# A gated scan feeding a two-level mixture of experts: the first fp32 job's transposes and first four matmuls set behind the sixth unit's ranking

## The chip, the cores and the metric

The kernel runs on one core of a Trainium2 chip. The metric is the device time of one execution in microseconds (us). Three executions of the kernel before took 760.2, 761.58 and 762.66 us; their median is 761.58 us. One further execution was profiled.

## The reference, cut to what matters

Four sequences of 3648 tokens with 256 channels go through a gated scan. Each of the 14592 results is routed to one of 4 groups and then to one of the 4 experts of that group (top 1 both times), and that expert's two-layer network is applied, scaled by the two softmax weights.

```python
sig = 1.0 / (1.0 + np.exp(-f_logit))
f = lower_bound + (1.0 - lower_bound) * sig
i = 1.0 - f
for t in range(S):
    h = f[:, t] * h + i[:, t] * x[:, t]
    y[:, t] = h
...
g_idx = argmax(x @ w_group);  g_w = softmax(...)[g_idx]
e_idx = argmax(x @ w_expert[g]);  e_w = softmax(...)[e_idx]
h = np.maximum(x @ w1[g, e], 0.0)
out = g_w * e_w * (h @ w2[g, e])
```

## The kernel before

**Phase 1, by units.** The tokens are cut into 29 units of 512 (the last is shorter). For unit u: ScalarE computes the gate, a tanh (`p1_tanh`, L211, instruction L218) and two affine steps that turn it into f (`p1_affine`, L228); VectorE multiplies the input by 1 - f (`p1_gate`, L265, for the early units; inside `p1_tb`, L244, for later ones) and scans each half of the channels (`p1_tb(u, 0)` and `p1_tb(u, 1)`, L255, 512 steps each). TensorE then computes the router's logits (`p1_router`, L302), ScalarE copies them (L307), TensorE turns them (L315) and ScalarE copies the result Lg (L316). VectorE picks group and expert in small steps called s1, s2 and f3, the last of which writes the one-hot tile oh16f (L406); ScalarE takes an exponential (`f4x`, L426); TensorE ranks the tokens within their experts by small matmuls (`f4`, L417, L418, L420); VectorE sums the exponentials (`s6`, L361 first) and forms the positions posi (`f5`, L431 and L433), after which ScalarE copies the running counts (L435). `p1_back` transposes the scanned unit on TensorE (L283, 8 transposes) and ScalarE copies it out into rows (L285, twice, and L287); GpSimd scatters the rows into per-expert lists in DRAM (L392, four per unit). The first eight units are ranked one by one, so "unit 5" is the sixth.

**Phase 2, by jobs.** A job applies one expert to some rows of its list. Its rows are loaded by SyncE (xr, L924), transposed on TensorE (L1007), copied by ScalarE (xh and xl, L1013), multiplied by w1 (`m1_step`; the first three jobs run in fp32 by `raw1`, L1041), passed through a ReLU (L1044) and multiplied by w2 (`m2_step`, `raw2`, L1076). One call of `m1_step` of the first job covers two of the eight hidden blocks: four fp32 matmuls of 128x256, each of which the profile shows as two records. The second products of the first job, and the transposes of the second job, are tied behind the ranking of unit 7 (`BEHIND[2] = 7`, `tc.issue_after(ranked[...])`).

**What orders the work.** Phase 1 is a list of thunks made by `p1_thunks`; marks are positions in that list. The order on SyncE's queue is that of the program throughout. On TensorE, VectorE and ScalarE it is that of the program only inside the block `tc.manual_schedule(...)` at the end of the function: there the thunks up to the mark "first" are run, and then the first job's preparation (its transposes with `keep_warm`, and the copies xh and xl). What is traced later (the loop over jobs, which calls the remaining thunks between the matmul steps by `bg_step`) is placed by a scheduler that works with a cost model and may also put it into gaps of the block. `tc.keep_in_program_order` ties one instruction behind the one traced before it on its engine; `pinned` does so for the tanh and the gate of units 8 to 10. Unit 11's input is loaded early (`LAST_AT`), and its tanh is not tied.

`keep_warm(bank, n)` issues n matmuls of bf16 128x128 whose result nobody reads; `job_xt` of the first job issues 12 ahead of its transposes. PSUM tiles with the tag "p" rotate over three banks and those with "m1" over three.

In the round u = 6 the thunks are, in this order: router(5), logits(5), gate(6), scan (6, 0), the binding of the group, tanh(7), s1, the exponential, s2, f3, the ranking f4, affine(7), back(5), s6, f5 with the reciprocals, the scatters, the mark "first", scan (6, 1), `place(6)` and `choose(6)`.

Of the kernel before, what the change touches and what calls it, by code (L numbers as in the profile page):

```python
# [30 lines left out]
FAST = 9  # L31
# [9 lines left out]
AHEAD = 3  # L41
STAGED = range(4, 8)
BEGIN = 6
BEHIND = {2: 7, 3: 7}
MT = -(-max(CAPS) // 128)
QUARTERS = (13, 14, 15)
# [6 lines left out]
def gated_scan_moe(ctx: ExitStack, tc, zx, lower, wroute, wexp, out, S):  # L53
# [151 lines left out]
        units[u] = {"z": zt[:, 0], "x": zt[:, 1]}  # L205

    def pinned(u, ins):
        if 8 <= u <= FAST + 1:
            tc.keep_in_program_order(ins)

    def p1_tanh(u):  # L211
# [233 lines left out]
    def p1_thunks(us, groups, parts):  # L445
        th, marks = [], {}
# [21 lines left out]
        def put(f):  # L468
            th.append(f or (lambda: None))
            if hasattr(f, "mark"):  # L470
                marks[f.mark] = len(th)
# [28 lines left out]
        for u in us + [us[-1] + 1]:  # L500
            seq = []
            if u <= FAST:
# [12 lines left out]
                if ending:  # L515
                    bind, bound, (s1, f4x, s2, f3, f4, s6, f5, s7s) = routing(u - 1)
                    if u - 1 == BEHIND[2]:
                        f4.mark = "ranked"
                    put(bind)
                    if u > BEGIN:  # L520
                        back(u - 1)
                    put(lambda u=u: p1_tanh(u + 1))
                    put(s1)
                    put(f4x)
                    if u > 1 and member[u - 2] == member[u - 1]:
                        back(u - 2)
                    put(s2)
                    put(f3)
                    put(f4)
                    wave(u, 1)  # L530
                    put(lambda u=u: p1_affine(u + 1))
                    back(u - 1)
                    put(bound)
                    put(s6)
                    put(f5)
                    for f in s7s:
                        put(f)
                    wave(u, 1)
                elif u > 7:
                    wave(u, 1)  # L540
                    back(u - 1)
                for m in [m for m, v in ROWS_AT.items() if u == v]:
                    f = lambda m=m: early_rows(m)
                    f.mark = m
                    put(f)
                if u == BEGIN:
                    f = lambda: None
                    f.mark = "first"
                    put(f)
                put(lambda u=u: p1_tb(u, 1))  # L550
                wave(u, 1 if u < FAST else 99)
                if u in cuts and u - 1 in ends:
                    put(lambda u=u: place(u))
# [267 lines left out]
    def make_job(kind, idx):  # L821
# [22 lines left out]
        j.wh, j.wl, j.st = {}, {}, {}  # L844
        j.hh, j.hl = {}, {}
        j.xh, j.xl = {}, {}
        return j

    def job_e(j):
# [103 lines left out]
    def job_xt(j, pi):  # L953
# [2 lines left out]
        c0 = b0 - j.chunks[ch][0]  # L956
        if j.raw:
            if j.idx == 0:
                keep_warm(bank("m2"), 12)
            j.xh[ch] = mo.tile([P, 2 * P], F32, name="xh", bufs=X_BUFS)  # L960
            j.xl[ch] = mo.tile([P, 2 * P], F32, name="xl", bufs=X_BUFS)
        elif c0 == 0:
            j.xh[ch] = mo.tile([P, KD, 2 * P], F16, name="xh", bufs=X_BUFS)
            j.xl[ch] = mo.tile([P, KD, 2 * P], BF16, name="xl", bufs=X_BUFS)
# [168 lines left out]
    def first_parts():  # L1133
# [10 lines left out]
            out += [(u, f) for f in fs]  # L1144
        return out

    thunks, marks = p1_thunks(list(range(NU)), GROUPS, first_parts())
    bgq = deque(thunks)
    done = [0]
# [82 lines left out]
    with tc.manual_schedule(engines={mybir.EngineType.PE, mybir.EngineType.DVE, mybir.EngineType.Activation}):  # L1232
        start_macro(len(PLAN))
        bg_to(marks["first"])
        for t in prep_thunks(macros[len(PLAN)][0]):
            t()
    pending = None
    for mi, mac in enumerate(macros):
        if mi < len(PLAN):
# [7 lines left out]
        for j in mac:  # L1247
            for ch in range(len(j.chunks)):
                for cs in j.cols[ch]:
                    m1_step(j, ch, cs)  # L1250
                    left -= len(cs)
                    bg_step(q, left - 2, len(cs))
                for pj, pc in ([pending] if pending else []) + ([(j, ch)] if j.raw else []):
# [75 lines left out]
```

## Time and profile before

| | |
|---|---|
| median of three executions | 761.58 us |
| the profiled execution, its own time | 760.23 us |
| its span in the profile | 758.4 us |
| TensorE busy | 718.3 us (95%) |
| VectorE busy | 531.1 us (70%) |
| ScalarE busy | 450.3 us (59%) |
| GpSimd busy | 296.0 us (39%) |

Between the span and the execution's own time lie 1.83 us that the trace does not cover. Times in the rows are counted from the start of the span. A granted clock of 1.00 stands for the upper level of TensorE's clock (2.4 GHz) and 0.50 for the lower (1.2 GHz).

### The profile page before, as it was taken

The page shows a single profiled execution, that of the slowest core. Times are in us where ns is not written, and L with a number is a line of the kernel's source. Part 1 is how long each engine was busy: PE and PEld are TensorE (multiplying, and loading weights), DVE is VectorE, ACT ScalarE, POOL GpSimd, SP SyncE. Part 2 cuts the span into 40 slices and gives each one's busy share as a digit, 9 for nine tenths or more (in the row PEclk, how much of TensorE's full clock was granted, in tenths as well). Part 3 has the DMA queues.
Part 4 walks back from the last instruction along what each step waited for, and adds up shares of the span by engine and source line. Part 5 has one row for each costly group of instructions (what it writes and reads, how often), then busy time and mean ns, then how long its engine had stood idle before and what let it go on. Part 6 is the DMA issues. An engine that isn't in the chain of part 4 may idle for free.

```text
span 758.4 us, 21398 instructions
## 1 busy us (share of the span) xinstructions
PE 718.3 (95%) x8115; PEld 638.5 (84%) x8115; DVE 531.1 (70%) x1155; ACT 450.3 (59%) x824; POOL 296.0 (39%) x273
## 2 busy tenths in 40 slices
PE   3669999999999999999999999999999999999995
PEld 1557888888888888898899899999899999999995
DVE  6998779999999985687455735463754675557652
ACT  6667778876886864445454534453544465556552
POOL 3656355566855663631122212222222222223223
PEclk9969999999999999999999999999999999999998
DMA  8988899998897854567885752424354455566521
GB/s 326 397 276 278 249 378 336 382 298 294 300 315 248 251 177 149 131 178 181 187 201 155 161 129 77 133 83 122 120 143 107 142 164 139 159 177 196 172 70 35
DMA packets 101384, 152.01 MB, mean 200 GB/s; under 512 B 60898, under 2 KB 70913, under 8 KB 98464
## 3 DMA queue, kind: packets, MB, share of 16 engines
q1 hardware_dynamic: 86752, 103.27, 47.3%
q0 software_dynamic: 11408, 30.02, 10.8%
q10 hardware_dynamic: 3120, 17.34, 6.8%
q8 instruction: 64, 1.05, 0.6%
q14 instruction: 40, 0.33, 0.2%
HBM read 112.66 MB, written 38.40 MB: 199 GB/s over the span
## 4 chain that ended last, share of the span: by engine, by line
PE 62%; DVE 19%; DMA 8%; issue 4%; ACT 3%; SPq 1%; POOL 1%; POOLq 0%; ACTq 0%; DVEq 0%
PE ps_m L1095 30%; PE ps_m L1063 6%; PE ps_m L1065 6%; PE ps_m L1064 6%; DVE h L255 4%; DVE w L951 4%; PE ps_p L1063 3%; DMA st<-in_wexp_dram 3%; PE ps_p L1065 3%; PE ps_p L1064 3%; DVE hl L1069 3%; DMA xs<-rows,posi 3%; PE ps_p L283 1%; DVE zt L244 1%; ACT w L949 1%
## 5 line engine op out<-in xcount | busy, mean ns | idle before, releaser
L1095 PE MATMUL ps_m<-w,hh 128*128 128x256 bf16 (+7 forms) x2480 | 304.2, 251 | 0.0
L1095 PE MATMUL ps_m<-w,hl 128*128 128x256 f16 (+3 forms) x1240 | 250.3, 251 | 0.0
L1095 PEld LDWEIGHTS <-hh 128*128 128x128 f16 (+4 forms) x2480 | 183.1, 99 | 21.2 <-issue 2.7
L1063 PE MATMUL ps_m<-xh,w 128*128 128x256 f16 (+10 forms) x782 | 187.4, 254 | 4.7 <-DVE hl L1069 4.7
L1065 PE MATMUL ps_m<-xh,w 128*128 128x256 f16 (+10 forms) x782 | 187.2, 254 | 0.0
L1064 PE MATMUL ps_m<-xl,w 128*128 128x256 bf16 (+10 forms) x782 | 187.2, 254 | 0.0
L392 POOL DMA_INDIRECT xs<-rows,posi x114 | 141.1, 1238 | 111.3 <-ACT rows L287 25.6
L951 DVE TENSOR_TENSOR w<-st,w 128x1024 bf16<-128x1024 f32 x116 | 140.1, 1219 | 52.8 <-ACT w L949 52.5
L1109 POOL DMA_INDIRECT out_dram<-o,info x71 | 83.7, 1179 | 233.2 <-ACT o L1107 203.1
L1069 DVE SCALAR_TENSOR_TENSOR hl<-ps_m,hh 128x512 bf16<-128x512 f32 (+9 forms) x166 | 109.7, 666 | 57.2 <-ACT hh L1068 56.9
L1068 ACT ACTIVATE hh<-ps_m 128x512 f16<-128x512 f32 (+9 forms) x166 | 97.4, 588 | 65.3 <-PE ps_m L1065 64.9
L949 ACT CAST w<-st 128x1024 f16<-128x1024 f32 x116 | 120.4, 1050 | 14.1 <-PE ps_m L1095 8.1
L1064 PEld LDWEIGHTS <-w 128*128 128x128 f16 x1088 | 106.5, 98 | 12.4 <-issue 5.4
L1063 PEld LDWEIGHTS <-w 128*128 128x128 f16 x1088 | 106.5, 98 | 8.4 <-issue 1.2
L1065 PEld LDWEIGHTS <-w 128*128 128x128 bf16 x1088 | 106.4, 98 | 7.1 <-issue 0.2
L1095 PEld LDWEIGHTS <-hl 128*128 128x128 bf16 (+3 forms) x1240 | 97.7, 99 | 10.1 <-issue 0.7
L1109 POOL DMA_INDIRECT out_dram<-o,meta x51 | 59.9, 1175 | 104.8 <-ACT o L1107 93.7
L1107 ACT ACTIVATE o<-ps_m,info 128x256 f32<-128x256 f32 (+4 forms) x71 | 31.6, 445 | 73.6 <-PE ps_m L1095 65.8
L1069 DVE SCALAR_TENSOR_TENSOR hl<-ps_p,hh 128x512 bf16<-128x512 f32 (+13 forms) x65 | 41.9, 644 | 42.4 <-ACT hh L1068 42.1
L1063 PE MATMUL ps_p<-xh,w 128*128 128x256 f16 (+17 forms) x306 | 71.5, 249 | 0.0
L1064 PE MATMUL ps_p<-xl,w 128*128 128x256 bf16 (+17 forms) x306 | 71.5, 249 | 0.0
L1065 PE MATMUL ps_p<-xh,w 128*128 128x256 f16 (+17 forms) x306 | 71.5, 249 | 0.0
(179 smaller groups left out, 821.1 us busy)
## 6 DMA issues: line engine op xcount, KB each, us to landing
st<-in_wexp_dram SPq DMA_DIRECT2D x116, 512.0 KB, 7.6
zt<-in_zx_dram ACTq DMA_DIRECT2D x16, 1024.0 KB, 7.4
xs<-blank SPq DMA_DIRECT2D x28, 258.0 KB, 8.0
zt<-in_zx_dram SPq DMA_DIRECT2D x6, 1024.0 KB
w<-in_wexp_dram SPq DMA_DIRECT2D x12, 512.0 KB, 9.6
st<-in_zx_dram SPq DMA_DIRECT2D x8, 512.0 KB, 13.6
xr<-xs SPq DMA_DIRECT2D x14, 258.0 KB, 3.2
xs<-rows,posi POOLq DMA_INDIRECT x114
```

The lines of the kernel that those rows point to most:

```text
L255: sn = nc.vector.tensor_tensor_scan(out=h[:, k, c0 - a:c1 - a], data0=ff[:, k, c0 - a:c1 - a], data1=uu[:, k, c0 - a:c1 - a], initial=init ...
L392: sc = nc.gpsimd.indirect_dma_start(out=xs_v[G["t0"] + t][:, :], out_offset=bass.IndirectOffsetOnAxis(ap=R["posi"][:, t:t + 1], axis=0), i ...
L949: nc.scalar.copy(j.wh[i], j.st[i])
L951: nc.vector.tensor_tensor(out=j.wl[i], in0=j.st[i], in1=j.wh[i], op=ALU.subtract)
L1063: nc.tensor.matmul(po, w1_at(j.wh, k, c), xh[:, k], start=(k == 0), stop=False)
L1064: nc.tensor.matmul(po, w1_at(j.wh, k, c), xl[:, k], start=False, stop=False)
L1065: nc.tensor.matmul(po, w1_at(j.wl, k, c), xh[:, k], start=False, stop=(k == KD - 1))
L1068: eviction[0] = nc.scalar.activation(hi, pv, AF.Relu).ins
L1069: nc.vector.scalar_tensor_tensor(out=j.hl[ch][:, cs[0]:cs[-1] + 1, 0:w], in0=pv, scalar=0.0, in1=hi, op0=ALU.max, op1=ALU.subtract)
L1095: nc.tensor.matmul(pm[i * q:i * q + n, 0:dw], h[ch][:, c, ts], w2_at(w, c)[:, i * dw:(i + 1) * dw], start=(c == 0 and s == 0), stop=(c == ...
L1107: nc.scalar.activation(o[s, 0:dw], pm[s, 0:dw], AF.Copy, scale=lt.bitcast(F32)[s, r, 1:2])
L1109: nc.gpsimd.indirect_dma_start(out=out_v[out_n[0]].rearrange("n (g d) -> (n g) d", g=g), out_offset=bass.IndirectOffsetOnAxis(ap=lt[s, r, ...
```

## The change

Three things are edited. First, in the round u = 6 the transposes and copies of unit 5 (`back(5)`) come ahead of tanh(7) instead of behind affine(7). Second, the mark "first" moves up to just behind affine(7), so that the first job's preparation, now with 20 dummy matmuls, is traced directly behind unit 5's ranking and affine(7); the thunks from s6 of unit 5 to scan (6, 1), and one new thunk, `first_step`, follow it up to a new mark "begin", all still inside the manual block. `first_step` runs the first `m1_step` of the first job (four matmuls and a ReLU), which the loop over jobs then leaves out. Third, `pinned` also covers unit 11.

```diff
+BACKS = 5
...
     def pinned(u, ins):
-        if 8 <= u <= FAST + 1:
+        if 8 <= u <= FAST + 2:
             tc.keep_in_program_order(ins)
...
                     put(bind)
-                    if u > BEGIN:
+                    if u > BACKS:
                         back(u - 1)
                     put(lambda u=u: p1_tanh(u + 1))
...
                     put(lambda u=u: p1_affine(u + 1))
+                    if u == BEGIN:
+                        f = lambda: None
+                        f.mark = "first"
+                        put(f)
                     back(u - 1)
                     put(bound)
                     put(s6)
...
+                put(lambda u=u: p1_tb(u, 1))
                 if u == BEGIN:
+                    put(first_step)
                     f = lambda: None
-                    f.mark = "first"
+                    f.mark = "begin"
                     put(f)
-                put(lambda u=u: p1_tb(u, 1))
...
             if j.idx == 0:
-                keep_warm(bank("m2"), 12)
+                keep_warm(bank("m2"), 20)
...
+    def first_step():
+        j = macros[0][0]
+        j.begun.append((0, j.cols[0][0]))
+        m1_step(j, *j.begun[-1])
...
         for t in prep_thunks(macros[len(PLAN)][0]):
             t()
+        bg_to(marks["begin"])
...
                 for cs in j.cols[ch]:
-                    m1_step(j, ch, cs)
+                    if (ch, cs) not in j.begun:
+                        m1_step(j, ch, cs)
```

## Rows read from the trace of the kernel before

**Rows 1.** Busy time by stretch: PE, PEld, DVE, ACT, POOL, clock, DMA share, GB/s

```profile
70.00:80.00 10.00, 10.00 (x67) 8.62 (x66) 9.91 (x18) 4.78 (x10) 6.71 (x5) 1.00 0.94 355
...
150.00:160.00 10.00, 10.00 (x105) 9.21 (x103) 10.00 (x23) 9.36 (x18) 5.61 (x4) 1.00 0.97 304
...
380.00:420.00 40.00, 40.00 (x416) 36.41 (x414) 22.66 (x37) 20.13 (x34) 8.23 (x8) 1.00 0.73 184
```

**Rows 2.** The same view, microsecond by microsecond

```profile
48.00:49.00 1.00, 0.69 (x2) 0.47 (x3) 0.96 (x2) 0.43 (x3) 1.00 (x1) 0.50 0.00 0
...
56.00:57.00 1.00, 1.00 (x5) 0.51 (x3) 1.00 (x3) 0.00 (x0) 0.69 (x2) 0.50 1.06 415
...
58.00:59.00 1.00, 1.00 (x10) 0.85 (x8) 0.75 (x2) 0.45 (x2) 0.82 (x1) 1.00 0.99 386
```

**Rows 3.** Timeline of PE: start, duration, line, operation, idle before and its releaser

```profile
48.31 0.47 PE L315 MATMUL ps_p<-ident,rs 128*128 128x128 f32 x1 [0.39 <-ACT rs L307]
48.71 0.71 PE L417 MATMUL ps_p<-runoff,row 1*128 1x80 f32 x2
52.13 0.21 PE L418 MATMUL ps_p<-oh16f,upto 128*128 128x64 bf16 x1 [2.71 <-DVE oh16f L406]
...
52.33 1.95 PE L283 MATMUL ps_p<-ident,h 128*128 128x128 f32 x8
54.07 1.49 PE L292 MATMUL ps_m<-upto,tri 128*128 128x128 bf16 x12
55.35 0.42 PE L1007 MATMUL ps_p<-ident,xr 128*128 128x128 f32 x1
...
57.97 0.70 PE L1041 MATMUL ps_m<-xh,w 128*128 128x256 f32 x2
...
58.62 1.04 PE L283 MATMUL ps_p<-ident,h 128*128 128x128 f32 x8
...
68.09 0.19 PE L418 MATMUL ps_p<-oh16f,upto 128*128 128x64 bf16 x1
```

**Rows 4.** Timeline of ACT, same columns

```profile
48.94 1.06 ACT L218 ACTIVATE st<-st 128x1024 f32<-128x1024 f32 x1
49.90 1.05 ACT L218 ACTIVATE zt<-zt 128x1024 f32<-128x1024 f32 x1
51.09 0.27 ACT L426 ACTIVATE ex<-ge 128x80 f32<-128x80 f32 x1
51.27 1.50 ACT L228 ACTIVATE st<-st,mid,half 128x512 f32<-128x512 f32 x2
...
53.46 0.59 ACT L285 COPY rows<-ps_p 128x512 f32<-128x512 f32 x1
...
57.48 0.38 ACT L1013 COPY xl<-ps_p 128x256 f32<-128x256 f32 x1
```

**Rows 5.** Timeline of DVE, same columns

```profile
49.59 1.27 DVE L255 TENSOR_TENSOR_SCAN h<-st,h 128x512 f32<-128x512 f32 x1
...
51.85 0.23 DVE L406 TENSOR_TENSOR oh16f<-oh 128x64 bf16<-128x64 f32 x1
52.00 0.23 DVE L361 TENSOR_REDUCE sm<-ex 128x20 f32<-128x80 f32 x1
...
52.89 1.21 DVE L265 SCALAR_TENSOR_TENSOR st<-st 128x1024 f32<-128x1024 f32 x1
...
57.44 1.21 DVE L244 SCALAR_TENSOR_TENSOR zt<-zt 128x1024 f32<-128x1024 f32 x1
...
59.07 0.24 DVE L329 TENSOR_REDUCE mx<-Lg 128x20 f32<-128x80 f32 x1 [0.32 <-ACT Lg L316]
```

**Rows 6.** The chain that ended last, just behind unit 7's ranking

```profile
68.37 0.58 PE ps_p L1007 x4
68.95 1.30 PE ps_m L1041 x6
```

**Rows 7.** Issues on SP's queue, the first job's rows

```profile
48.31 0.89 SPq L924 DMA_DIRECT2D xr<-xs  x2
```

More of the change, by code (lines that the diff above doesn't have):

```diff
@@ L846, in make_job @@
         j.xh, j.xl = {}, {}
+        j.begun = []
         return j
```

## The prediction

> **What bounds the kernel now.** I read the busy time by stretch first. Where a saving early on is worth anything is seen there: from 60 us on TensorE has no time to spare. It is busy for 10.00 of 10 us at 70 to 80, and for 40.00 of 40 at 380 to 420, where VectorE has 22.66; only between about 130 and 260 us is VectorE as full, 10.00 of 10 at 150 to 160, with the DMA engines at 0.97 [rows 1]. So a microsecond of TensorE work done earlier should come off the end, less what the VectorE stretch swallows.
>
> The timeline of TensorE comes next. Before 58 us the engine waits for phase 1: 2.71 us ahead of unit 5's ranking at 52.13, for oh16f [rows 3]. From there it runs without a gap: 8 transposes of unit 5, 12 dummies, the first job's transposes from 55.35, and the first real matmul of a job at 57.97 [rows 3]. The same view microsecond by microsecond shows the lower clock in all this: granted 0.50 at 48 to 49 and still at 56 to 57, and 1.00 at 58 to 59 [rows 2]. Between, at some 57.8, it rose, after TensorE had been busy for 5.6 us (57.8 - 52.13). Eight transposes took 1.95 us at the lower level and 1.04 at the upper [rows 3].
>
> The timelines of VectorE and ScalarE show who sets the pace up to 68 us. VectorE's chain from Lg of unit 6 at 59.07 [rows 5] to unit 7's ranking at 68.09 [rows 3] is 9.0 us long. That ranking is a gate: the first job's second products stand behind it. What TensorE still had to do of the first products when the gate opened is 1.30 us, beside 0.58 of the second job's transposes, which the gate holds too [rows 6].
>
> **The change part by part.** *Unit 5's transposes first.* They follow the logits (48.31 + 0.4 = 48.7) into a gap where TensorE waited anyway, and take 1.95 us at the lower clock: to 50.65. The first ranking matmuls (0.71) follow, to 51.3 [rows 3]. TensorE loses nothing by it.
>
> *Scan (6, 1) leaves the middle of s1.* The scheduler had put it there at 49.59 for 1.27 us [rows 5]. The pitch of such scans is 1.2, so oh16f comes at 51.85 - 1.2 = 50.65, done at 50.9, and the ranking runs at 51.3 instead of 52.13: 0.8 us earlier.
>
> *ScalarE's order.* It is the price. The second copy of unit 5's rows (0.59 long, one every 0.5) waits for the transposes' end at 50.65 and is over at 51.2. Only then comes tanh(7), which had started at 48.94 and takes 1.06: to 52.2. Unit 5's exponential, at 51.09 before, follows at 52.2, done at 52.45, and affine(7) (1.50) ends at 53.9 [rows 4]. The sum sm needs the exponential, so VectorE, done with oh16f at 50.9, stands until 52.45: 1.55 us idle where it had no gap. Behind sm (before: 52.00 to gate(7) at 52.89 [rows 5], plus 0.3 of two small steps that had slipped behind the gate) come 1.2 us to 53.7, then scan (6, 1) to 54.95, then gate(7), due at 52.89 before: 2.06 us later.
>
> *Unit 11 in its place.* Its tanh at 49.90 [rows 4] and gate of 1.21 at 57.44 [rows 5] leave this stretch. The gate goes into the stretch after 75 us; I cost it there at nothing, because TensorE is the full engine there and ScalarE has 4.78 of 10 us [rows 1]; if that cover is gone the price is 1.2 us. Here it gives 1.2 back. Unit 6's s1 then stands at 59.07 - 0.32 (the wait shown) + 2.06 - 0.3 - 1.2 = 59.3, or 0.2 later than before, if Lg is there by then.
>
> *Twenty dummies and the first job's transposes.* Twelve dummies go from 54.07 to 55.35, 0.107 us each [rows 3]; twenty take 2.14, from the ranking's end at 51.6 to 53.75. Four transposes take 0.98 at the lower clock, 0.5 at the upper. Their rows were issued by SP from 48.31 on, 0.89 long [rows 7], which leaves 4.5 us to land; that they had landed by 55.35 is all that the timeline of TensorE shows. The first job's weights lie ready: no DMA engine moved anything at 48 to 49 [rows 2]. The copies xh and xl (0.38, about 0.3 apart [rows 4]) follow to 55.25, and the first matmul can start on xh at about 54.95 instead of 57.97: 3.0 us earlier.
>
> *The clock.* TensorE is now busy without a gap from 48.31 on. [...] These take 8 records of 0.217 (1.30 for 6 [rows 6]), 1.73 us, and twice that, 3.46, at the lower level. I take the upper, because it is what the nearest row shows, and keep both.
> The Trainium skill's page "TensorE: Matmul & The Clock Gate" (Part 1: The HAM clock gate) says that the moment of the transition differs from run to run, because it depends on where the first matmul happens to land. By that rule the step costs 1.73 us in some executions and 3.46 in others. The rise at 57.8 is one instance here and cannot show it.
>
> *Four matmuls ahead of router(6).* With them, router(6) starts at about 56.7, Lg is out at 58.0, and s1 does not wait for it (59.3). At the lower clock they end at 58.4, router(6) at twice its time at 59.5, and Lg is out at 60.6.
>
> *GpSimd and SP.* No instruction is added to either. Unit 5's scatters need its copies and the reciprocals, about 1 us earlier than before; the second job's rows wait for them on SP, and its transposes for the gate at 68.09: worth nothing. On SP nothing changes places around the block.
>
> **The sum.** TensorE starts real matmuls 3.0 us earlier, but before the gate it has only 1.30 us of first products left to bring forward [rows 6]; the rest of the lead becomes idle time in front of the gate. The gate itself moves by the 0.2 of unit 6's s1, less some 0.4 that the chain lost to matmuls queued ahead of its rankings (of 0.32 in one wait and more of that size): -0.2, with bounds of -1.2 (one scan's pitch, if the scheduler leaves scan (8, 1) out of unit 7's s1 as well) and +1.4 (the lower clock in the item above: 60.6 + 0.1 against 59.3). Together -1.5. Of this I let the stretch with VectorE full swallow 0.3, between nothing and all of it: -1.2 us. The profiled execution had a span of 758.4 and took 760.23 us, so its like would take 759.0; it stands 1.35 below the median of the runs, and the forecast is made against the median: 761.58 - 1.2 = 760.4 us. A measurement of this kernel can tell about 0.3% from no change, 2.3 us, so this counts as the same.
>
> **Rivals.** *A: the gate comes early (faster).* With TensorE warm and the scheduler free to order anew, the whole lead of 3.0 us arrives at the gate. Then the time is about 761.58 - 3.0 = 758.6, up to 1 us less if scan (8, 1) leaves s1 too. For it: VectorE's chain is freed of unit 11, and units 6 and 7 are short of Lg (0.32). Against: the 1.55 us that VectorE stands. Chance 0.30.
>
> *B: the chain is the bound, and it is late (slower).* VectorE's stand of 1.55 us is not made good by unit 11's gate, because that work is wanted later, and the clock rises only after the four matmuls, so that router(6) stands behind 3.46 us of them. Then Lg comes at 60.6 and the gate by 1.5 later; with the 1.2 us of unit 11's gate wanted back in a full stretch it is +2.7: 764.3. It decides once unit 6's s1 starts later than about 60.6. For it: the lower clock up to 57.8. The rule of the page "TensorE: Matmul & The Clock Gate" of the Trainium skill (above) would give it in part of the executions. Against: VectorE's idle time after 75 us, while TensorE is full. Chance 0.18.
>
> *C: hidden anyway (same).* The first job's start is no bound at all: the stretch from 130 to 260 us is set by VectorE and the transfers, and the lead is idle time there: 761.6. For it: 10.00 of 10 us and 0.97 [rows 1]. Against: TensorE has no time to spare there either. Chance 0.12. That the change doesn't do what it says (the first four matmuls still after 57 us, because the copies xh and xl come late) ends here too.
>
> **How the numbers follow.** Forecast 0.40, A 0.30, B 0.18, C 0.12. Faster by over 0.3% is A, 0.30; within 0.3% is the forecast and C, 0.52; slower is B, 0.18. The range reaches from 757.4, A with most of what a scan adds, to 763.6, which leaves out the worse part of B; the forecast's own range is 759.3 to 761.8.
>
> **What would show it.** Right: the ranking of unit 5 near 51.3, VectorE idle for about 1.5 us ahead of sm near 52.4, twenty dummies to 53.8, a granted clock of 1.00 by 55, the first job's first matmul near 55, and TensorE idle ahead of unit 7's ranking at about 68. Wrong: sm not waiting for the exponential; a first matmul after 57; unit 7's ranking before 66.5 or after 69.5; or a difference between the two kernels that arises after 100 us, where the change touches nothing, from another order of the scheduler's.

## The result, and the profile after

The changed kernel takes 766.27 us (median of 19 runs, 761.22 to 770.65), the kernel before 760.84 beside it (19 runs, 759.36 to 763.23): a ratio of 1.007, 95% interval 1.0057 to 1.0084. It is slower by about 5.4 us. Its runs also scatter over 9.4 us, those of before over 3.9. The profiled execution took 766.32 us with a span of 764.5; all times below are of that one, unless another kernel is named. The kernel's lines carry numbers one to seven higher than before (L315 is now L316, L924 is L931, L1007 is L1014, L1041 is L1048).

Around the block the change does what it says. The timeline of PE, answering to [rows 3], with three stops from later on that the kernel before does not have:

```profile
47.41 0.47 PE L316 MATMUL ps_p<-ident,rs 128*128 128x128 f32 x1 [0.39 <-ACT rs L308]
47.67 1.91 PE L284 MATMUL ps_p<-ident,h 128*128 128x128 f32 x8
...
50.17 0.19 PE L419 MATMUL ps_p<-oh16f,upto 128*128 128x64 bf16 x1 [0.19 <-DVE oh16f L407]
...
50.31 1.28 PE L293 MATMUL ps_m<-upto,tri 128*128 128x128 bf16 x20
...
54.23 0.70 PE L1048 MATMUL ps_m<-xh,w 128*128 128x256 f32 x2
...
67.62 0.19 PE L419 MATMUL ps_p<-oh16f,upto 128*128 128x64 bf16 x1 [0.87 <-DVE oh16f L407]
...
68.98 1.35 PE L1083 MATMUL ps_m<-w,hh 128*128 128x256 f32 x5
...
112.88 0.74 PE L1014 MATMUL ps_p<-ident,xr 128*128 128x128 f32 x4 [2.30 <-ACT rows L286]
...
126.40 0.48 PE L1014 MATMUL ps_p<-ident,xr 128*128 128x128 f32 x2 [2.46 <-DMA xr<-xs]
128.29 1.10 PE L1014 MATMUL ps_p<-ident,xr 128*128 128x128 f32 x4 [1.41 <-ACT rows L288]
```

The transposes of unit 5 fill the gap, the first job's first matmul stands at 54.23 instead of 57.97, and the gate (unit 7's ranking) opens at 67.62 instead of 68.09 [rows 3]. What follows the gate in the chain that ended last is now

```profile
67.90 0.58 PE ps_p L1014 x4
...
69.05 2.36 PE ps_m L1083 x10
```

and the 1.30 us of first products that stood there [rows 6] are gone. The clock, microsecond by microsecond, answering to [rows 2]; granted clock, DMA share and GB/s are the last three columns:

```profile
49.00:50.00 1.00, 0.98 (x5) 0.59 (x4) 0.86 (x5) 0.83 (x3) 0.70 (x2) 0.70 0.53 145
50.00:51.00 1.00, 0.83 (x18) 0.83 (x19) 0.12 (x1) 1.00 (x2) 0.72 (x1) 1.00 0.40 136
```

It is at its upper level from 50 us on, and not at 57.8. ScalarE first, then VectorE, for [rows 4, 5]:

```profile
50.11 1.06 ACT L219 ACTIVATE st<-st 128x1024 f32<-128x1024 f32 x1
51.06 0.26 ACT L427 ACTIVATE ex<-ge 128x80 f32<-128x80 f32 x1
```

```profile
51.36 0.23 DVE L362 TENSOR_REDUCE sm<-ex 128x20 f32<-128x80 f32 x1 [1.24 <-ACT ex L427]
...
58.63 0.23 DVE L330 TENSOR_REDUCE mx<-Lg 128x20 f32<-128x80 f32 x1
```

So at 69 us the changed kernel leads by 1.77 us: the first of the first job's second products stands at 68.98, and in the kernel before at 70.75.

```profile
70.75 1.56 PE L1076 MATMUL ps_m<-w,hh 128*128 128x256 f32 x6
```

Of this lead 0.90 us is there already at the logits of unit 5 (47.41 against 48.31), ahead of everything that the change edits. In e6, a second trace of the changed kernel, these logits stand at 48.27, and the lead is 0.85 us (69.90).

**Where the time goes** is seen in the busy time by stretch, answering to [rows 1]: PE, PEld, DVE, ACT, POOL, clock, DMA share, GB/s.

```profile
70.00:80.00 10.00, 10.00 (x68) 8.44 (x67) 8.70 (x11) 7.74 (x16) 7.27 (x6) 1.00 1.02 345
...
110.00:120.00 10.00, 6.98 (x59) 5.58 (x58) 8.77 (x23) 8.34 (x17) 5.67 (x6) 1.00 1.03 414
120.00:130.00 10.00, 6.12 (x41) 5.04 (x40) 9.72 (x16) 9.26 (x16) 5.78 (x4) 0.90 1.01 371
```

and in the same stretches of the kernel before:

```profile
110.00:120.00 10.00, 10.00 (x74) 8.38 (x73) 8.69 (x23) 8.04 (x16) 7.54 (x7) 1.00 1.02 402
120.00:130.00 10.00, 9.47 (x102) 8.07 (x101) 9.16 (x19) 8.34 (x16) 4.55 (x4) 1.00 1.01 322
```

TensorE stands for 6.9 us between 110 and 130 (10 - 6.98 and 10 - 6.12), where it stood for 0.5 before. Setting the n-th of TensorE's matmuls of the jobs (6258 records in either trace) beside the n-th of the other trace tells when the loss is made. The one that starts at 97.4 us in the kernel before starts 1.83 us earlier in the changed one, so the lead is kept up to there; the one at 118.8 starts 0.5 us later, the one at 124.5 7.2 later, and from 146 us on it is 5.9 to the end. ScalarE's copies of the experts' products (into hh, hl and o; 371 in either trace) say the same from the 24th on: 6.2 us behind (139.36, 133.19), and 5.9 from the 45th (185.21, 179.27; the 301st 647.38, 641.42). Nothing is lost after 140 us. Part of it is the clock, which falls with the stops:

```profile
126.00:128.00 2.00, 0.48 (x2) 0.32 (x2) 1.86 (x5) 2.00 (x4) 0.54 (x1) 1.00 1.02 413
128.00:130.00 2.00, 1.71 (x8) 1.47 (x9) 2.00 (x3) 1.52 (x5) 1.22 (x1) 0.52 1.00 395
130.00:132.00 2.00, 2.00 (x14) 1.49 (x12) 2.00 (x5) 0.18 (x2) 0.00 (x0) 0.62 0.88 352
```

After 4.4 us with 0.48 of work (123.9 to 128.3) TensorE runs at a granted 0.52 and 0.62, and its records of 0.27 us take 0.42. At the upper level the busy time of the last two rows would have been 1.6 us shorter ((1 - 0.52) x 1.71 + (1 - 0.62) x 2.00).

The transposes that wait there belong to the fifth job, and what they wait for is its rows. Issues on SP's queue, after and then before (xr: rows of the third and fourth jobs at 82 us, of the fifth job and the next at 117 to 120; st: weights, the fourth job's first):

```profile
81.64 3.68 SPq L931 DMA_DIRECT2D xr<-xs  x4
90.18 1.48 SPq L684 DMA_DIRECT2D xs<-blank  x2
91.94 20.23 SPq L948 DMA_DIRECT2D st<-in_wexp_dram  x11
120.26 3.09 SPq L931 DMA_DIRECT2D xr<-xs  x4
```

```profile
82.00 3.56 SPq L924 DMA_DIRECT2D xr<-xs  x4
88.22 1.49 SPq L678 DMA_DIRECT2D xs<-blank  x2
89.97 19.39 SPq L941 DMA_DIRECT2D st<-in_wexp_dram  x11
116.74 3.10 SPq L924 DMA_DIRECT2D xr<-xs  x4
```

The transposes for which the fifth job's rows are used run without a stop in the kernel before:

```profile
122.44 0.88 PE L1007 MATMUL ps_p<-ident,xr 128*128 128x128 f32 x6
```

The rows of the third and fourth jobs are issued at the same time, but the blanks behind them, which must not overwrite what is still being read, come 2.0 us later, so do the weights behind the blanks, and the fifth job's rows come 3.5 later. SP stands 6.8 us for the scatters of units 8 and 9 before it issues these rows (6.1 before). GpSimd issues the last two of the eight at 107.34 and 109.38, against 105.24 and 107.17, after a stand of 5.06 us (4.23) for ScalarE. ScalarE's timeline, after and then before:

```profile
81.48 0.23 ACT L317 COPY Lg<-ps_p 128x80 f32<-128x80 f32 x1 [0.39 <-PE ps_p L316]
84.37 0.34 ACTq L205 DMA_DIRECT2D zt<-in_zx_dram  x1
84.76 1.06 ACT L219 ACTIVATE zt<-zt 128x1024 f32<-128x1024 f32 x1 [3.06 <-DVE oh L340]
...
88.33 0.35 ACT L427 ACTIVATE ex<-ge 128x160 f32<-128x160 f32 x1
```

```profile
79.85 0.33 ACTq L204 DMA_DIRECT2D zt<-in_zx_dram  x1
80.29 0.47 ACT L1107 ACTIVATE o<-ps_m,xr 128x256 f32<-128x256 f32 x1 [3.14 <-DMA w<-in_wexp_dram]
...
83.72 0.22 ACT L316 COPY Lg<-ps_p 128x80 f32<-128x80 f32 x1
...
86.47 0.35 ACT L426 ACTIVATE ex<-ge 128x160 f32<-128x160 f32 x1
```

ScalarE issues the input load of unit 13 from its own queue and stands in front of it for some 3 us in both kernels. Before, the stand ends at 79.85, when weights have landed, ahead of the logits of units 8 and 9 (83.72). In the changed kernel these logits are out 2.2 us earlier (81.48), but the stand lies right behind them, and the exponential comes 1.9 us later, 88.33 against 86.47. The records of the transfers in the traces say why. The transfers of SP and ScalarE between 60 and 127 us share eight semaphores (counters that tell that a transfer has landed), and a transfer waits for the one that had its semaphore before. In the kernel before the load of unit 13 has the semaphore of the last weights of the third job, issued at 66.37; in the changed kernel, whose transfers are issued in another order, it has that of the second of the third job's row transfers, which SP issues only at 82.21.

### The profile page after: what moved, and what is told of

It reads as the page before. It is cut to its first block, busy times and chain, and to the rows that moved or that the text cites. A ratio compares the mean times of both kernels' runs of the same rounds, so it can differ in the third digit from the quotient of the medians.

```text
span 764.5 us, 21414 instructions
## 1 busy us (share of the span) xinstructions
PE 719.1 (94%) x8123; PEld 638.3 (83%) x8123; DVE 531.3 (69%) x1155; ACT 450.1 (59%) x824; POOL 295.9 (39%) x273
## 3 DMA queue, kind: packets, MB, share of 16 engines
q8 instruction: 64, 1.05, 0.6%
## 4 chain that ended last, share of the span: by engine, by line
PE 63%; DVE 17%; DMA 6%; issue 5%; ACT 4%; POOL 2%; SPq 2%; POOLq 0%; DVEq 0%; ACTq 0%
PE ps_m L1102 30%; PE ps_m L1070 7%; PE ps_m L1071 6%; PE ps_m L1072 6%; DVE h L256 4%; PE ps_p L1070 3%; DVE w L958 3%; PE ps_p L1071 3%; PE ps_p L1072 3%; DMA st<-in_wexp_dram 2%; DVE hl L1076 2%; PE ps_p L284 2%; DMA out_dram<-o,meta 1%; DMA xs<-blank 1%; PE ps_m L1083 1%
```

## The experiments

Theories, as they were formed: **S**, ScalarE's stand at unit 13's load (at first called L); **P**, the tie of unit 11's tanh to program order; **W**, the start of the fourth job's weight casts; **O**, that the order of before is a lucky one; **X**, the chain from ScalarE over the scatters to the fifth job's rows; **D**, that from 100 us on the DMA engines are full, so what they leave undone before is missing later. Ratios are to the kernel before, timed in the same group of runs. The runs stand in five groups (e1 to e4, e5 to e8, e9 to e12, e13 to e16, e17 and e18); the kernel before takes 761 us in the second and the last and 780 to 784 us in the other three. A ratio is good within a group; times and traces are compared with those of before and after only in the groups at 761 us.

| run | what it is | before, us | ratio, 95% interval |
|---|---|---|---|
| e1_load13_early | change, unit 13's load early | 780.5 | 1.0034 (1.0010 to 1.0057) |
| e2_no_pin | change without the tie | 780.5 | 1.0080 (1.0048 to 1.0111) |
| e3_before_pin | before with the tie alone | 780.5 | 1.0075 (1.0048 to 1.0102) |
| e4_no_first_step | change, first four matmuls not moved | 780.5 | 1.0074 (1.0048 to 1.0099) |
| e5_before_control | before | 761.4 | 0.9999 (0.9984 to 1.0013) |
| e6_after_again | change | 761.4 | 1.0058 (1.0038 to 1.0078) |
| e7_before_load13_late | before, unit 13's load later | 761.4 | 1.0000 (0.9988 to 1.0012) |
| e8_step_only | first job's early start alone | 761.4 | 1.0033 (1.0018 to 1.0048) |
| e9_after_loads_on_sp | change, two loads on SP | 783.0 | 1.0030 (0.9999 to 1.0060) |
| e10_no_pin_loads_on_sp | the same without the tie | 783.0 | 1.0065 (1.0039 to 1.0091) |
| e11_before_loads_on_sp | before, two loads on SP | 783.0 | 0.9993 (0.9968 to 1.0019) |
| e12_after_loads_early | change, two loads early | 783.0 | 1.0077 (1.0049 to 1.0106) |
| e13_after_weights_first | change, weights ahead of blanks | 783.7 | 1.0076 (1.0049 to 1.0103) |
| e14_before_weights_first | before, weights ahead of blanks | 783.7 | 1.0023 (0.9991 to 1.0055) |
| e15_before_cast4_late | before, one weight cast later | 783.7 | 1.0017 (0.9987 to 1.0048) |
| e16_after_third | change | 783.7 | 1.0118 (1.0078 to 1.0158) |
| e17_before_scalar_held | before, ScalarE held 3.1 us | 761.5 | 1.0019 (1.0000 to 1.0039) |
| e18_load13_early_again | e1 again | 761.5 | 1.0044 (1.0025 to 1.0062) |

**One part taken out, or alone (e1 to e4, e8).**

```
e1   -  seq += [lambda u=u: (p1_load(u + AHEAD - 1), ...
     +  seq += [lambda u=u: ([p1_load(v) for v in ((12, 13) if u == 10 else (u + AHEAD - 1,))], ...
e2   -  if 8 <= u <= FAST + 2:          + if 8 <= u <= FAST + 1:
e3      the kernel before with FAST + 2, and nothing else
e4   -  put(first_step)                 + pass
e8      e2, and BACKS = 6 instead of 5
```

> The changed kernel with one line moved: the load of unit 13's input is traced one round earlier, together with unit 12's. In the built program it then stands ahead of the tanh of unit 11 on ScalarE's queue, and the transfer that it must wait for is a blank written at 67 us, no longer the rows of the third job. All edits of the change stay. Theory L (the load of unit 13 stands on ScalarE's queue behind the third job's rows, issued at 81.6 us and landed at 84.3, and holds up all that follows): the load goes out by 78 us, ScalarE no longer stands from 81.7 to 84.4, the fourth job's last weights are cast by 109 us instead of 112.3, TensorE is idle for under 2 us between 110 and 130 instead of 7, and the time is 757 to 761 us. Theory W (the early first job only empties TensorE's work sooner, and the transfers set the time) and theory P (unit 11's late tanh and gate cost it): nothing of theirs is touched, and the time stays at 764 to 768.

> The changed kernel without the third edit: the tanh of unit 11 is free again. The built program puts the load of unit 13 behind a blank written at 67 us. Theory P: the time comes back to 759 to 762, and with unit 11's tanh back at about 50 us the gate and the affine steps leave the stretch from 75 us on. Theory L: back to 757 to 761 too, because the load no longer waits for the third job's rows; the load goes out before 80 us. Theory W: stays at 764 to 768, because the first job starts just as early.

> The kernel before with the third edit alone (unit 11's tanh keeps its place). The built program puts the load of unit 13 behind unit 12's load, which goes out near 69 us. Theory P: slower by 4 to 6 us, 765 to 767. Theory L: 759 to 762, no loss, because the load does not wait for the third job's rows. Theory W: 760 to 762, as the first job starts as late as before.

> The changed kernel without the new thunk: the first four matmuls are left to the scheduler, all else stays (transposes ahead, twenty dummies, unit 11 tied). The built program puts the load of unit 13 behind unit 12's load. Theory L: 757 to 761, with the load out before 80 us. Theory P: 764 to 768. Theory W: the transposes and copies still come early and the scheduler puts the first matmuls right behind them, so it stays near 764 to 768.

> The changed kernel without the earlier transposes of unit 5 and without the tie on unit 11's tanh: the first job's start after unit 6's rank matmuls, with twenty dummies, is alone. Theory P (the tie on unit 11 costs) expects no loss: 0.997 to 1.001. A fourth theory, O (the order of before is a lucky one, and every other order of ScalarE's queue between 70 and 100 us costs about as much), expects 1.005 to 1.008, as with the pin alone and with the change without the pin.

No part carries the loss. The tie alone costs 0.75% (e3), the change without it 0.80% (e2), the change without the moved matmuls 0.74% (e4), the early start alone 0.33% (e8). These don't add up to 0.7%. P is not excluded as a part, but as the only cause it falls with e8, which has no tie. O predicted 1.005 to 1.008 for e8, and got less.

The traces add that e2, e3 and e4 lose time at another place than the changed kernel does. From the logits of unit 5 to the first of the first job's second products it is 21.57, 21.63 and 21.62 us in after, e6 and e18, 22.45 in the kernel before and 22.20 to 22.58 in the seven traces that start like the kernel before (before, e5, e7, e11, e14, e15, e17). In e2, e3 and e4 it is 24.02, 26.55 and 24.08, and in e12 and e16 further down 25.36 and 24.63: up to 4.1 us more than in the kernel before, ahead of 78 us, where the changed kernel gained. In e3 TensorE stands ahead of unit 6's logits, in e16 in front of the first real matmul:

```profile
62.40 0.33 PE L315 MATMUL ps_p<-ident,rs 128*128 128x128 f32 x1 [1.60 <-issue]
```

```profile
58.42 0.70 PE L1048 MATMUL ps_m<-xh,w 128*128 128x256 f32 x2 [2.59 <-ACT xh L1020]
```

Behind these stops the granted clock falls to 0.50 (from 64 to 68 us in e3, from 60 to 62 in e16). Why these executions stand there stays open. The ratios of these five runs hold this loss, as far as their one trace each tells, and say the less about the one between 110 and 130 us.

**Controls (e5, e6, e16).** The kernels before and after, unedited.

> The kernel before itself, for a trace on the chip on which the variants run. Every theory expects a ratio of 1.000. What is read from it: when unit 13's input load starts on ScalarE, when the exponential of units 8 and 9 runs, when the fourth job's weights are issued, and how long TensorE is idle between 110 and 140 us. If the theory holds that a chain from those units' logits to the fourth job's weights sets the time, all variants timed so far (ratios 1.003 to 1.008) must have the weights' casts 1.5 to 4 us later than this trace.

> The changed kernel itself beside its variants. Every theory expects about the ratio on record, 1.006 to 1.008. What is read from it: whether the load of unit 13 stands at the head of ScalarE's queue until the third job's rows have landed here too, and whether the loss of TensorE lies between 110 and 130 us again.

> The changed kernel beside these variants, for the comparison on the same chip. Every theory expects 1.006 to 1.008; W expects its fourth cast at 111 us or later.

e6 is the most telling trace, because the same program was slower: span 768.3 against 764.5. ScalarE's timeline names the transfer that it stands for:

```profile
87.52 0.33 ACTq L205 DMA_DIRECT2D zt<-in_zx_dram  x1
87.90 1.06 ACT L219 ACTIVATE zt<-zt 128x1024 f32<-128x1024 f32 x1 [5.27 <-DMA xr<-xs]
...
91.46 0.35 ACT L427 ACTIVATE ex<-ge 128x160 f32<-128x160 f32 x1
```

The stand is 2.2 us longer than in the first trace, the exponential 3.1 later, the fifth job's rows are issued at 122.39 (2.1 later), and TensorE stops for them for 3.91 us at 130.53 and runs at 0.50 to 0.57 until 136. The 45th copy is 3.2 us later, of which 0.9 are there already at the second products (69.90 against 68.98). The other 2.3 go with the chain X, within one program, in this one pair of executions. That the stand now hangs on a transfer that takes longer in one execution than in another also fits the scatter of the runs.

**The stand moved or imitated (e7, e17, e18).**

```
e7   before: p1_load(13) traced at u == 12 instead of 11
e17  before: + for _ in range(3 if u == 12 else 0):
             +     nc.scalar.copy(ff[:, :, 0:w], U["z"][:, :, 0:w])      (ahead of unit 12's tanh)
e18  e1 unchanged
```

> The kernel before with one thing changed: unit 13's input load follows unit 12's tanh on ScalarE's queue instead of going ahead of it. Theory L (the load of unit 13, and what waits for it, sets the time) expects a ratio of 1.002 to 1.005, since the load goes at least one tanh (1.06 us) later. Theory P (the work put ahead of the exponential of units 8 and 9 sets it) expects 1.000 to 1.002, since only one tanh changes its place. Theory W (the fourth job's weights set it) expects the ratio to follow the time at which these weights are issued: 1.000 if that has not moved, 1.005 or more if it is 2 us late.

> The kernel before with three copies of 1.05 us (unit 12's gate input onto itself) ahead of unit 12's tanh on ScalarE: ScalarE is held about 3.1 us ahead of the exponential of units 8 and 9, as by the stand at unit 13's load in the changed kernel; which load waits for which transfer stays as it was, and so do TensorE's lead and unit 11. Theory X (ScalarE late at 82 to 88 us makes the exponential and the row copies of units 8 and 9 late, by these their scatters, by these the fifth job's rows on SP; TensorE stops for these rows at 124 to 128 us, and its clock falls) expects the exponential and the issue of the fifth job's rows 2 to 3.5 us later than before and a ratio of 1.002 to 1.006. If the ratio is 1.000 or below with the rows that late, X falls, and the loss needs TensorE's lead or the tie on unit 11 as well. P expects 1.000.

> The changed kernel with unit 13's load traced beside unit 12's, so that it waits for a blank write and not for the third job's rows; ScalarE does not stand at it. It is timed a second time, beside the held kernel. X expects the loss of the changed kernel (1.006 to 1.008) to be smaller by what the exponential of units 8 and 9 gains: 1.000 to 1.004. P expects 1.006 to 1.008.

e7 was no test: unit 12's tanh took the place of the load, stood 2.88 us there, and the load went at 80.15 instead of 79.93 in e5. The time didn't move.

e17 holds ScalarE: the exponential is at 89.46, 3.4 us later than in e5 (86.08), and the fifth job's rows are issued at 118.51, 1.3 later. The cost is 0.19% (0 to 0.39), 1.4 us of the 5.4; X expected 0.2% at least and the rows 2 to 3.5 us later. TensorE does not stop for them:

```profile
122.71 0.98 PE L1009 MATMUL ps_p<-ident,xr 128*128 128x128 f32 x6
```

e18 is the reverse: ScalarE does not stand at unit 13's load (it goes at 80.76), and the rows are issued as early as in the kernel before, at 117.84. Still TensorE stops twice at the same place:

```profile
126.00 0.47 PE L1014 MATMUL ps_p<-ident,xr 128*128 128x128 f32 x2 [1.84 <-ACT zt L229]
128.42 0.72 PE L1014 MATMUL ps_p<-ident,xr 128*128 128x128 f32 x4 [1.95 <-ACT rows L288]
```

The stop of 2.30 us at 112.88 is gone, and by the medians about a third of the loss (1.0044 against 1.0058 to 1.007; the intervals touch). The trace does not show it: TensorE stands 0.39 us at 85.13 and 1.02 us at 92.40 instead, the lead at the second products is 0.95 us and not 1.77, and this execution loses 6.3 us against the trace of before, where the changed kernel loses 5.9. The releasers named here are the last events ahead of the start; in the changed kernel the first of the two was the rows' landing. From issue to transposes it is 8.2 us in e18 (126.00 - 117.84) and at most 4.2 in e17 (122.71 - 118.51). Around the stop the DMA engines are about as full in all four traces that follow (0.97 to 1.05); what differs is how much they moved before 100 us. The stretch from 60 to 100 us, and around the stop, of before, e17, e18 and after, in this order:

```profile
60.00:100.00 40.00, 39.86 (x288) 33.03 (x288) 31.39 (x80) 27.96 (x64) 19.58 (x17) 1.00 0.83 263
...
124.00:128.00 4.00, 3.98 (x48) 3.17 (x47) 3.44 (x4) 4.00 (x9) 0.52 (x1) 1.00 0.99 372
```

```profile
60.00:100.00 40.00, 39.87 (x288) 32.76 (x287) 29.51 (x75) 30.11 (x66) 17.56 (x15) 1.00 0.78 260
...
124.00:128.00 4.00, 4.00 (x50) 3.34 (x47) 3.79 (x8) 4.00 (x8) 1.78 (x3) 1.00 0.97 382
```

```profile
60.00:100.00 40.00, 37.58 (x271) 30.67 (x272) 30.10 (x75) 28.41 (x63) 16.66 (x14) 1.00 0.79 236
...
124.00:128.00 4.00, 0.64 (x4) 0.31 (x2) 3.72 (x10) 4.00 (x7) 2.38 (x2) 1.00 1.05 408
```

```profile
60.00:100.00 40.00, 38.85 (x294) 32.52 (x293) 31.15 (x75) 28.22 (x64) 18.68 (x16) 1.00 0.76 233
...
124.00:128.00 4.00, 0.48 (x2) 0.32 (x2) 3.72 (x10) 4.00 (x7) 2.24 (x2) 1.00 1.01 381
```

From 60 to 100 us the kernel before moves 263 GB/s x 40 us = 10.5 MB, e5 254, e7 261 and e17 260 GB/s. With the early first job it is 9.3 MB in the changed kernel (233), 229 GB/s in e6, 236 in e18 and 235 in e8. The eight traces fall into two groups, and TensorE stands ahead of the fifth job's transposes in the second alone. From 100 to 120 us the engines are full in all of them (1.02 to 1.03, 379 to 408 GB/s), so 1.2 MB that did not go before would take 1.2 / 0.39 = 3.1 us there, an estimate. This is D, formed from the traces and after the runs, on eight of them. Two things speak against it as a law. In e6, of the second group, the first of the fifth job's rows took at most 3.8 us from issue to transposes (122.39 to 126.15). And in the groups at 780 us bytes and loss do not go together: e15 moves 238 GB/s from 60 to 100 us at a ratio of 1.0017, e13 beside it 257 at 1.0076.

**Two loads off ScalarE's queue, or early (e9 to e12).** In the kernel of each name:

```
-ZX_SP = 12
+ZX_SP = 14                                   (not in e12)
                 if u == FAST:
+                    put(lambda: [p1_load(v) for v in (12, 13)])
                     f = lambda: None
                     f.mark = "begun"
```

> The changed kernel with the input loads of units 12 and 13 issued by SP, ahead of the third job's rows, instead of by ScalarE; so unit 14's load no longer shares a semaphore with these rows either. Theory S (ScalarE's stand at a load that waits for the third job's rows, and the loads and weights that go late behind it, are the loss) expects no stand of ScalarE over 1 us between 80 and 95 us, unit 14's load before 86 us, at least 19.6 MB moved between 70 and 130 us (before: 19.9, after: 18.7), and a ratio of 0.996 to 1.001: the first job's lead of 1.8 us is kept or just spent. Theory P (the tie on unit 11's tanh) expects 1.004 or more, since the tie is still there.

> The same loads on SP, in the changed kernel without the tie on unit 11's tanh. Theory S expects the same ratio as with the tie, 0.996 to 1.001. Theory P expects it clearly below the run with the tie, by 0.004 or more.

> The kernel before with the same loads on SP. Theory S expects 0.998 to 1.002, since before's loads stood behind weights that landed early enough. If earlier loads are worth something by themselves, whatever the first job does, this one is below 0.997; then a gain of the changed kernel with these loads is not the first job's.

> The changed kernel with the loads of units 12 and 13 still on ScalarE's queue but ahead of the third job's rows in program order: unit 13's load waits for a blank write, unit 14's still for the third job's rows. Theory S expects about half of the loss, 1.002 to 1.004, with unit 14's load after 88 us, behind or beside the fourth job's weights. Theory P expects the whole loss, 1.006 to 1.008.

e11 says that early loads are worth nothing by themselves. e9 got 1.0030, where S expected 1.001 at most; the changed kernel itself was not timed in this group (1.0058 to 1.0118 in others), so what the moved loads give back is not shown. e9 and e10 did not take the stand away either: ScalarE stands 3.90 us at the next load instead, unit 14's, which goes at 81.81 and 82.56. e12 has no stand at unit 13's load and keeps the loss, but by its trace it lost 2.9 us ahead of the second products (25.36 against 22.45). e12, almost the same program as e1, got 1.0077 where e1 got 1.0034, and e1 needs 21.31 us for that stretch; a single ratio of this kind is not to be leaned on in these groups.

**Weights and casts (e13 to e15).**

```
e13, e14   -  if ready[0]:
           +  if ready[0] and not 12 <= pptr[0] < 16:
                  ready[0] = False
                  blanks()
e15  before: + for _ in range(3 if j.idx == 3 and i == 3 and j.kind == "A" else 0):
             +     nc.scalar.copy(j.wh[3], j.st[2])
                  nc.scalar.copy(j.wh[i], j.st[i])
```

> The changed kernel with the two blank writes that follow the third and fourth jobs' rows on SP put behind the fourth job's four weight loads, so that these loads no longer wait for those rows to land. Theory W (the time follows the start of the fourth job's fourth weight cast, at about 1 us per us) expects the weights issued 3 to 6 us earlier, the fourth cast before 108.5 us, and a ratio of 0.997 to 1.001. Theory S (ScalarE's stand at unit 13's load) expects the same only if the stand is gone too: this load's semaphore now belongs to a blank write, so a stand below 1 us and a ratio below 1.004 by S. If the fourth cast is early and the ratio is still 1.006 or more, W falls.

> The kernel before with the same order on SP. W expects it to be faster only so far as its fourth cast is earlier than 107.7 us and TensorE was idle for it: TensorE of before is idle for 1.8 us in all between 90 and 160 us, so 0.997 to 1.000. S expects 1.000, there is no stand to remove.

> The kernel before with three more copies of 1.04 us on ScalarE ahead of the fourth job's fourth weight cast, and nothing else changed up to there: the cast starts 3.1 us or a little more later, at about 111 to 112 us. W expects a ratio of 1.003 to 1.006, as in the runs whose fourth cast starts at that time. S and P expect 1.000 to 1.002, since nothing before 107 us is changed.

In e15 the fourth cast starts behind three copies, at 115.86, 3.9 us later than the place of the first copy (111.92), for 0.17% with an interval that holds 0 (0.9987 to 1.0048). At 1 us per us, 3.9 us would be 0.50%, which lies just outside, so W as such a law is hardly left: in the first twelve runs the ratio went along with that cast, and the cast need not have caused it. e13 and e14 were no test of the weights: two more blanks now stood ahead of the third job's rows, which went at 89.33 instead of 85.54 (e16), so that the weights went at 92.57 instead of 93.72, and not 3 to 6 us earlier; and ScalarE stood 4.45 us at unit 13's load for a blank. The loss was smaller than in e16, the intervals touch.

## Why the prediction was wrong

**What held, and what was luck.** The steps up to the first matmul held, counted from the logits of unit 5, which were out 0.9 us earlier in this execution (47.41 against 48.31; e6 has 48.27). The ranking of unit 5 was foreseen 3.0 us behind them and came after 2.76, the first real matmul 6.6 us behind them and came after 6.8 (54.23). VectorE stood 1.24 us ahead of sm (1.55). The first products left behind the gate are 0, as assumed. The gate is 0.47 us earlier where 0.2 was forecast, but that is the head start of 0.9: counted from the logits it is 0.4 later. The 0.4 us that VectorE's chain was to win back did not come (from unit 6's s1 to the gate 8.99 us, 9.02 before). So it is luck in part that the second products, 1.77 us earlier, met the 1.5 of the sum; in e6 they are 0.85 earlier. The twenty dummies took 1.28 us instead of 2.14, since the clock was up by 50 us and the sum had costed them at the lower level; the first four matmuls ran at the upper level, as it took them. When the clock rises is not settled by the runs: in e18, whose order is the same up to there, it rose at 54.1.

**What failed** is what stands behind the sum.

- 'So a microsecond of TensorE work done earlier should come off the end.' TensorE was full between 70 and 130 us in the kernel before, but the DMA engines were full as well, 1.01 to 1.04 from 90 us on, and the rows that the prediction shows skip that stretch. The fifth job's rows were issued at 116.74 and used at 122.44 without a stop. A lead ends there: these rows wait for the scatters of units 8 and 9, and a matmul of the jobs that is done earlier does not make them land sooner. The lead of 1.77 us was still there at 97 us (1.83) and was spent in the stops from 112.88 on.
- 'On SP nothing changes places around the block', and GpSimd and SP costed at nothing. Around the block it is so. Thirty us later it is not: the load of unit 13 goes at 84.37 instead of 79.85, the fourth job's weights 2.0 us later, the fifth job's rows 3.5 us later. The scheduler orders the whole program anew, and the semaphore that a load shares changes with the order. This is the term that the sum put at nothing, and with it the sign of the whole was wrong: TensorE came to stand 5.9 us longer. How much of that each of the late transfers has, the experiments leave open.
- 'Unit 11 in its place ... I cost it there at nothing, because TensorE is the full engine there and ScalarE has 4.78 of 10 us.' ScalarE went to 7.74 at 70 to 80. Mean busy time was the wrong view: ScalarE issues loads and stands at them, and those stands are in no busy time. The tie alone costs 0.75% (e3), 5 to 6 us; the price that the prediction named if the cover were gone was 1.2 us. In e3's trace, though, 4.1 us are lost ahead of 78 us, so this run does not show that the cover after 75 us was missing.

**The rivals.** B had the sign, and not the mechanism: unit 6's s1 came at 58.63, far from the 60.6 at which it was to decide, and the first four matmuls ran at the upper clock. C is the nearest: it said that transfers make the lead idle time, but at 130 to 260 us and for no loss. The stretch from 160 to 260 us is the same in both kernels to 0.01 us of TensorE (97.61 and 97.60). The sign that the prediction listed last, a difference that arises after 100 us from another order of the scheduler's, is the one that came, and no chance had been given to it.

**The account of the 5.9 us** in the trace, over the same 670 records of TensorE in both, from the first of the second products (70.75 and 68.98) to 150.60 and 156.54: TensorE stands 7.70 us instead of 1.81, which is 5.9 more, and is busy for 79.86 us instead of 78.04, 1.8 more, of which 1.6 are the lower clock; less the lead of 1.77: 5.9. Of the standing, 2.3 us (at 112.88) lie behind ScalarE's queue: the transposes wait for a row copy at 112.25, that stands behind two casts, which stood 1.46 and 0.74 us for weights. This stop is gone in e18; e5, the kernel before itself, has one of 1.33 us at the same place. Another 3.9 (2.46 and 1.41) stand ahead of the fifth job's transposes, the first of the two for its rows; at the second the rows are named in e6 and a row copy of ScalarE here.

**Shown, and not shown.** Shown are the place and the size of the loss, that TensorE waits there for the fifth job's rows among full DMA engines, that the stand of ScalarE is real and hangs on the third job's rows (5.27 us in e6), and that holding ScalarE alone costs 1.4 us (0 to 3). That taking the stand out gives back a third rests on medians whose intervals touch. That the 1.2 MB of the DMA engines are the rest is argued from eight traces that fall into two groups; no run changed it by itself, and the traces at 780 us do not bear it out. So the cause of the larger part stays open. Open is why they move less from 60 to 100 us as soon as the first job starts early: in e8, which has neither the tie nor a stand for rows, the third and fourth jobs' rows are issued at 84.32 us against 81.06 in e5, behind the scatters, and the weights follow at 91.40 against 88.96. Why the tie alone costs as much is open too; by its one trace it loses 4.1 us at the first job's start. None of the runs is faster than the kernel before by more than its interval.

## What to carry to other kernels

Where a scheduler orders the program, the price of an edit is not settled in the block that it touches: list the transfers that compute engines issue from their own queues, and for each the transfer that it shares a semaphore with; a changed order can put it behind one that is issued much later. Before counting a microsecond of the full engine as a gain, look for the next stretch in which the DMA engines are full, and ask what the edit does to the bytes moved ahead of it. Parts of an edit that are timed alone need not lose at the place where the whole loses: look into each one's trace for that before adding them up. And before a lead is booked as forecast, count it from the last instruction that the edit does not touch, and in a second execution.

## What the runs showed of the hardware

- The DMA engines carry 379 to 408 GB/s at a share of 1.02 to 1.03 between 100 and 120 us in the eight traces at 761 us, while at 70 to 80 us the same share of 1.02 was 345 GB/s in the changed kernel and 290 in e8, and 0.94 was 355 in the kernel before. The share is time, not bytes.
- TensorE's clock came up by 50 us, with the engine busy without a pause since 47.41; in the kernel before it stayed at the lower level until 57.8, with pauses up to 52.13 and none after. It fell to 0.52 after the stops at 124 to 128 us. The Trainium skill ("TensorE: Matmul & The Clock Gate", Part 1: The HAM clock gate) says that the moment of the transition differs from run to run. The traces agree: in the one program of e1 and e18 the clock came up 1.3 us behind the logits of unit 5 in e1 (52.1 and 50.81) and 5.9 us behind them in e18 (54.1 and 48.17), while after and e6, again one program, have 2.2 and 2.1.
- The same kernel before takes 760.8 to 761.5 us in some groups of runs and 780.5 to 783.7 in others, at the same granted clock (0.98 to 0.99 over a run in the groups at 761 us, 0.97 to 1.00 in the others); the record names the same chip for e1 to e4 (780.5) and for e5 to e8 (761.4). So a difference of 0.3% is told only beside the kernel before in the same group.
